# A fused convolution and expert layer: where one expert's sums are loaded, when kept weights, chunk stores, sends and ranks stand in the plan

## The chip, the core and the metric

One core of a Trainium2 chip runs the kernel: TensorE (PE, with PEld for its weight loads), VectorE (DVE), ScalarE (ACT), GpSimd (POOL) and SyncE (SP), which work in parallel and each take their own instructions strictly in order. The metric is the device time of one execution in microseconds (us); less is better. Transfers are issued by SP and ACT (direct ones) and by POOL (indirect ones, with a row number for each row).

## The reference

28672 rows of 192 numbers go through two stages.

```python
w = softmax(weight_gen, axis=-1)                       # (8, 3584, 8 heads, 7 taps)
out = einsum('bshk,bskhg->bshg', w, x_unf)             # causal convolution with 7 taps, own weights for each row
x = out.reshape(28672, 192)
do_compute = x @ w_skip > 0
e_idx = argmax(x[do_compute] @ w_gate)                 # one of 8 experts
h = maximum(xc[mask] @ w1[e], 0.0)                     # 192 -> 1024
y[mask] = gate_w[mask, None] * (h @ w2[e])             # 1024 -> 192
out[do_compute] = xc + y
```

## The kernel before, in words

The convolution runs in 64 steps of 448 rows; four steps make a chunk of 1792 rows, and there are 16 chunks. A step has two `band` multiplications on DVE (L356, from `rot`, the softmaxed taps), `conv` on PE (L375), copies on ACT (L382), transposes on PE (`back`, L390) and copies into `acc` on ACT (L404, L406). After the fourth step of a chunk, `logits` (L413), `choose` on DVE (L428 to L452, which ends with the one-hot tiles `oh` and `rc`), `rank` on PE (L463 to L467) and `place` on DVE (L482 to L502) give every row its place in the bucket of its expert. `answer` (L508) stores the whole chunk in the output from SP, and 16 `send` scatters by POOL (L515) write the chunk's rows into the buckets.

The expert part works on pairs of 128-row tiles. `fetch` loads a pair's rows (`xg`, L653) and, after the first eight pairs, its expert's weights (L667); `prep_rows` splits and transposes the rows (L680 to L708); `up` and `down` (L718, L738) are the matmuls; `put` (L749) scatters the results. The first eight pairs use the weights in the slot where an expert was prepared.

`prep_expert(e)` prepares an expert's weights in pieces, one piece at each token `P`: the largest absolute sums of the next expert's raw weights are measured on ACT (`measure`, L223), their 128x2 sums are written to DRAM from ACT's queue (`peaks`, L225), and two pieces later `spread` (L230) loads all sums back into every partition. One piece later `load_raw` loads the raw weights of the expert after that from ACT's queue (L209). The next `prep_expert` begins on DVE with the maximum over the loaded sums (L238) and a few small instructions, whose result scales the first weights on ACT (L252). `keep` (L277) stores a prepared expert in DRAM from SP, in three transfers, for later pairs.

`SEQ` is the plan: four strings, one for each step of a chunk, of one-letter tokens. The kernel walks them, and a token whose condition holds emits its instructions there; every engine keeps that order. `F` is a place of the expert pipeline: it moves the pair at work by half a stage, pops one scatter (`pop`), and deals five pending small DVE instructions. `R` emits `rank`, `r` what follows it, `W` starts `place`, `V` emits `answer`, `5` stores the taps to `img` (L344) and `4` loads them back as `rot` (L349), `x` loads the step's rows (L309), `s` emits `keep`, `D` emits `fetch`, `P` one piece of the preparation. Pairs begin at step 15 (`START`). When all chunks are placed and sent, the remaining pairs run alone.

Of the kernel before, what the change touches and what calls it, by code (L numbers as in the profile page):

```python
# [20 lines left out]
P = 128  # L21
B, S, D, H, K = 8, 3584, 192, 8, 7
G = D // H
# [33 lines left out]
]  # L57
# [11 lines left out]
FAST = 6  # L69
FIRST = 14  # L70
TT = 2
LAG = 2
# [4 lines left out]
def conv_moe_kernel(ctx, tc, x, wg, w_skip, w_gate, w, out):  # L77
    nc = tc.nc
# [15 lines left out]
    outs, unsent = [], []  # L94
# [110 lines left out]
    all_sums = spare.bitcast(F32)[:, 0:2 * P]  # L205
# [8 lines left out]
    def load_raw(e):  # L214
        if e < E:
            raws[e] = [load_part(e, i) for i in range(2)]
# [10 lines left out]
    def spread(e):  # L227
        if e < E:
            pk = peaks[e:e + 1, :]
            nc.sync.dma_start(all_sums, bass.AP(tensor=pk.tensor, offset=pk.offset, ap=[[0, P], [1, 2 * P]]))  # L230

# [47 lines left out]
    fresh, unkept = {}, []  # L279
    prepared, prepares = [0], [0]  # L280

    def prep_all():
        load_raw(0)
        yield
        measure(0, 0)
        yield
        measure(0, 1)
        load_raw(1)
        yield
        yield  # L290
        spread(0)
        yield
        for e in range(E):
            while e >= SLOTS and spent[0] <= e - SLOTS:
                yield
            yield from prep_expert(e)
            prepared[0] += 1
            yield
# [475 lines left out]
    step, tick = [0], [0]  # L774
# [103 lines left out]
    ffn = [None]  # L878
# [10 lines left out]
    n = dict.fromkeys("kOCGceKLlRrHhWiV", 0)  # L889
# [13 lines left out]
    def placed(c):  # L903
# [3 lines left out]
        n["i"] += 1  # L907

    def chosen(c):
        yield from choose(c)  # L910
        n["h"] += 1

    def assigned(own):
# [3 lines left out]
    def token(t, k):  # L917
# [6 lines left out]
        elif t == "F":  # L924
            advance(n["K"] > n["O"])
            for _ in range(FAST if not ffn[0] and n["i"] <= 3 else 1):
                pop()
# [7 lines left out]
        elif t == "s":  # L935
            if unkept and k >= FIRST:
                keep()
# [12 lines left out]
        else:  # L950
            i = n[t]
            c = i // NQ
# [11 lines left out]
                "H": lambda: (i < n["l"], lambda: chores.append(chosen(i))),  # L964
                "R": lambda: (i < n["h"], lambda: rank(i)),
                "r": lambda: (i < n["R"], lambda: rank_out(i)),
# [15 lines left out]
    with tc.manual_schedule():  # L982
# [33 lines left out]
        while n["V"] < NCHUNK or unsent or not last[0]:  # L1016
            k = n["k"]
# [63 lines left out]
```

## Time and profile before

| what | value |
|---|---|
| median of three runs | 983.23 us (978.15 to 986.6) |
| the profiled execution | 983.36 us, its span 981.6 us |
| PE busy | 803.0 us (82% of the span) |
| DVE busy | 663.9 us (68%) |
| ACT busy | 468.1 us (48%) |
| POOL busy | 398.3 us (41%) |
| mean granted TensorE clock | 0.927 |

PE is the busiest engine. Its busy share is low in the first third and high after it: the page gives it in 40 slices of 24.5 us as `0586534576767999898899989999998999999997`, and the clock that it was granted in the same slices as `9897566898888999999999999999998999999999`. So the views of single stretches tell more than the means.

### The profile page before, as it was taken

What the parts mean: (1) busy time and instruction counts of PE and PEld (TensorE: products, weight loads), DVE (VectorE), ACT (ScalarE), POOL (GpSimd) and SP (SyncE); (2) the same over time, 40 slices, a digit from 0 to 9 for tenths busy, and PEclk for the clock granted to TensorE, in tenths of its full rate; (3) what the DMA queues carried; (4) which work ended last, traced back from release to release, by engine and by line L of the source; (5) the groups of instructions that cost most, each with busy time, mean ns of one, the idle gap of its engine ahead of it and who ended that gap; (6) DMA issues with size and microseconds to landing.
All of it is one profiled execution on the core that took longest, in us unless ns stands there. A gap on an engine that the chain in (4) does not pass through costs nothing. (4 is left out here: it accounts for less than half of the span.)

```text
span 981.6 us, 36503 instructions
## 1 busy us (share of the span) xinstructions
PE 803.0 (82%) x15128; PEld 686.0 (70%) x15128; DVE 663.9 (68%) x1937; ACT 468.1 (48%) x1119; POOL 398.3 (41%) x417
## 2 busy tenths in 40 slices
PE   0586534776767999898899989999998999999997
PEld 0465323664656877687777877887886888889996
DVE  7597464866857688767668676867764666775553
ACT  1463352555544544455444555554544554454441
POOL 1028734142045544554254525352533545362222
PEclk9897566898888999999999999999998999999999
DMA  5957848867674849586676768674947384989990
GB/s 168 284 159 211 231 145 263 307 170 210 214 240 148 295 126 339 159 282 216 204 244 201 244 211 247 229 238 140 303 126 248 119 295 136 318 258 314 243 242 20
DMA packets 110793, 214.70 MB, mean 219 GB/s; under 512 B 28786, under 2 KB 68525, under 8 KB 108834
## 3 DMA queue, kind: packets, MB, share of 16 engines
q1 hardware_dynamic: 77794, 175.13, 54.7%
q10 hardware_dynamic: 15072, 15.48, 7.1%
q0 software_dynamic: 17760, 21.75, 7.1%
q8 instruction: 119, 1.95, 0.9%
q14 instruction: 48, 0.39, 0.1%
HBM read 141.37 MB, written 77.81 MB: 223 GB/s over the span
## 5 line engine op out<-in xcount | busy, mean ns | idle before, releaser
L515 POOL DMA_INDIRECT bucket<-acc,ixi x256 | 273.3, 1068 | 309.7 <-ACT hh L722 68.8
L718 PE MATMUL ph<-xT,wst 128*128 128x256 f16 x2280 | 297.3, 279 | 27.0 <-DVE hl L728 13.5
L718 PEld LDWEIGHTS <-wst 128*128 128x128 f16 x2280 | 220.4, 100 | 67.6 <-issue 28.5
L722 ACT ACTIVATE hh<-ph 128x512 f16<-128x512 f32 x228 | 135.7, 596 | 255.3 <-PE ph L718 241.3
L738 PE MATMUL py<-wst,hh 128*128 128x192 f16 x1824 | 249.0, 249 | 0.0
L738 PE MATMUL py<-wst,hl 128*128 128x192 f16 x912 | 226.7, 249 | 2.1 <-issue 1.9
L749 POOL DMA_INDIRECT out_dram<-xg x114 | 116.7, 1024 | 269.4 <-DVE xg L744 206.2
L728 DVE SCALAR_TENSOR_TENSOR hl<-ph,hh 128x512 f16<-128x512 f32 x228 | 155.2, 682 | 100.6 <-ACT hh L722 98.7
L356 DVE TENSOR_TENSOR bd<-rot,mask 128x896 f32<-128x896 f32 x128 | 137.3, 1081 | 62.8 <-PE bt L375 61.1
L375 PE MATMUL bt<-bd,xt 64*32 64x56 f32 x8192 | 128.9, 233 | 59.0 <-issue 23.0
L738 PEld LDWEIGHTS <-hh 128*128 128x128 f16 x1824 | 164.0, 99 | 17.5 <-issue 9.8
L375 PEld LDWEIGHTS bt<-bd,xt 64*32 64x32 f32 x8192 | 102.8, 113 | 92.8 <-issue 48.6
L390 PE MATMUL pa<-ident,xs 128*112 128x128 f32 x512 | 78.2, 299 | 25.1 <-ACT acc L404 10.9
L738 PEld LDWEIGHTS <-hl 128*128 128x128 f16 x912 | 90.2, 99 | 0.8 <-DVE hl L728 0.5
L390 PEld LDWEIGHTS pa<-ident,xs 128*112 128x112 f32 x512 | 64.0, 148 | 29.0 <-ACT xT L706 11.4
L744 DVE SCALAR_TENSOR_TENSOR xg<-py,fc,xg 128x192 f32<-128x192 f32 x114 | 42.2, 411 | 59.4 <-PE py L738 55.0
L382 ACT COPY xs<-bt 128x448 f32<-128x448 f32 x128 | 65.8, 539 | 31.6 <-PE bt L375 25.8
L706 ACT COPY xT<-pt 128x512 f16<-128x512 f16 x92 | 49.4, 589 | 43.1 <-PE pt L705 43.0
L689 ACT ACTIVATE xs<-xg,rs 128x192 f16<-128x192 f32 x114 | 45.5, 447 | 44.1 <-DVE rs L686 32.2
L404 ACT COPY acc<-pa 112x384 f32<-112x384 f32 x128 | 56.1, 482 | 8.9 <-PE pa L390 5.7
L705 PE MATMUL pt<-ident,xs 128*128 128x128 f16 x368 | 32.6, 227 | 22.3 <-DVE xs L695 8.8
L680 ACT ACTIVATE xs<-xg 128x192 f16<-128x192 f32 x114 | 40.2, 359 | 12.6 <-DMA xg<-bucket 10.7
(149 smaller groups left out, 700.0 us busy)
## 6 DMA issues: line engine op xcount, KB each, us to landing
wst<-wsp SPq DMA_DIRECT2D x98, 512.0 KB
wst<-wsp SPq DMA_DIRECT2D x49, 520.0 KB
xt<-in_x_dram SPq DMA_DIRECT2D x64, 384.0 KB
out_dram<-acc SPq DMA_DIRECT2D x16, 1358.0 KB
raw<-in_moe_w_dram ACTq DMA_DIRECT2D x16, 768.0 KB
xg<-bucket SPq DMA_DIRECT2D x57, 194.0 KB
wsp<-wst SPq DMA_DIRECT2D x16, 512.0 KB
rot<-img SPq DMA_DIRECT2D x16, 448.0 KB
```

Source lines behind the costliest of these rows:

```text
L356: nc.vector.tensor_tensor(bd.rearrange("p h (m u) -> p h m u", m=K), rot_[c][:, :, i0 * H:(i0 + 2) * H].rearrange("p m h -> p h m").unsque ...
L375: mm = nc.tensor.matmul(bt[a][GP * j:GP * (j + 1), c0:c0 + QH], xt[p0:p1, b0:b0 + GP], bd_[k, i // 2][p0:p1, i % 2 * H + h, :], start=True ...
L382: nc.scalar.copy(xs_[k][:, 2 * a:2 * a + 2, :], bt_[k][a][:, 0:2 * QB * QH].rearrange("p (x c) -> p x c", x=2))
L390: nc.tensor.transpose(pa[j][0:Q, x * P:(x + 1) * P], xs[:, x, j * Q:(j + 1) * Q], ident)
L404: nc.scalar.copy(acc_[c].rearrange("p (a b) d -> p a b d", a=2)[:, :, 2 * q + j, 0:D].rearrange("p a (h g) -> p a h g", g=G), pa[j][0:Q, : ...
L515: i = nc.gpsimd.indirect_dma_start(out=bviews[t], out_offset=bass.IndirectOffsetOnAxis(ap=rt_[c][:, t:t + 1], axis=0), in_=acc_[c][:, t, : ...
L706: nc.scalar.copy(xT[:, t], pt)
L718: mm = nc.tensor.matmul(ph[:, fi * 2 * P:(fi + 1) * 2 * P], wt[:, a * FF + f0:a * FF + f0 + P], xT[:, :, cc, :], start=j == 0, stop=j == 4)
L722: nc.scalar.activation(hh, ph, AF.Relu)
L728: nc.vector.scalar_tensor_tensor(hl, ph, 0.0, hh, op0=ALU.max, op1=ALU.subtract)
L738: mm = nc.tensor.matmul(py[:, t, 0:D], l[:, a], w2v[:, f, r, :], start=f == 0 and t == 0 and j == 0, stop=f == NFB - 1 and j == 2, skip_gr ...
L749: i = nc.gpsimd.indirect_dma_start(out=oviews[nsc[0] % 8], out_offset=bass.IndirectOffsetOnAxis(ap=xg[:, t0 + t, D + 1:D + 2].bitcast(I32) ...
```

## The change

Five things change. The load of the sums (`spread`) is issued from ACT's queue where it was SP's; for the first expert it also comes before the second expert's raw weights. Kept weights are stored from step 16 on (`KEEP`), where it was step 14 (`FIRST`, which still rules the pairs' assignment). `V` stands in the fourth string behind `4`, where it stood in the third ahead of `5`. A place pops two scatters while more than eight of a chunk are unsent. `R` waits until the place counter is past the one at which `choose` ended, by one place more when pairs are at work.

```diff
-    "x F C W r R a D P F G W r V P F W D 5 c b T M P F e P F P F D P s T M K O F P",
-    "x F C a D P F G 4 P F D c b T M P F e 0 P F P F D 1 P s T M K O F P",
+    "x F C W r R a D P F G W r P F W D 5 c b T M P F e P F P F D P s T M K O F P",
+    "x F C a D P F G 4 V P F D c b T M P F e 0 P F P F D 1 P s T M K O F P",
+KEEP = 16
-            nc.sync.dma_start(all_sums, bass.AP(tensor=pk.tensor, offset=pk.offset, ap=[[0, P], [1, 2 * P]]))
+            nc.scalar.dma_start(all_sums, bass.AP(tensor=pk.tensor, offset=pk.offset, ap=[[0, P], [1, 2 * P]]))
         measure(0, 1)
+        yield
+        spread(0)
+        yield
         load_raw(1)
-        yield
-        yield
-        spread(0)
         yield
     def chosen(c):
         yield from choose(c)
         n["h"] += 1
+        chosen_at[0] = tick[0]
-            for _ in range(FAST if not ffn[0] and n["i"] <= 3 else 1):
+            for _ in range(FAST if not ffn[0] and n["i"] <= 3 else 1 + (len(unsent) > 8)):
                 pop()
-            if unkept and k >= FIRST:
+            if unkept and k >= KEEP:
                 keep()
-                "R": lambda: (i < n["h"], lambda: rank(i)),
+                "R": lambda: (i < n["h"] and tick[0] > chosen_at[0] + (1 if ffn[0] else 0), lambda: rank(i)),
```

Line numbers of the kernel after are larger by one from L52 to L909, by three or four behind that.

The first place is ACT's order around the sums of expert 3 (`spare` is the tile that they are loaded into; `raw` here are the raw weights of expert 4). Before:

```order
L225 DMA peaks<-wm 128x2
L404 COPY acc<-pa 112x2x192 x2
L406 COPY ls<-pl 128x224
L459 ACTIVATE dl<-dl 112x128
L474 COPY qf<-rk 128x136
L209 DMA raw<-in_moe_w_dram 128x1536 x2
L382 COPY xs_2065<-bt 128x448
L252 ACTIVATE wst<-raw,wsc 128x1024
```

After, at the same place:

```order
L226 DMA peaks<-wm 128x2
L231 DMA spare<-peaks 128x256
L405 COPY acc<-pa 112x2x192 x2
L407 COPY ls<-pl 128x224
L460 ACTIVATE dl<-dl 112x128
L475 COPY qf<-rk 128x136
L210 DMA raw<-in_moe_w_dram 128x1536 x2
L383 COPY xs_2065<-bt 128x448
L253 ACTIVATE wst<-raw,wsc 128x1024
```

The load of the sums now stands on ACT, ahead of the raw weights and right behind the store that it waits for.

The second place is SP's order at steps 14 and 15, where the first pair's rows are fetched. Before:

```order
L508 DMA out_dram<-acc 112x3104
L344 DMA img_79<-wt 8x7x896 x2
L277 DMA wsp<-wst 128x2048 x2
L277 DMA wsp<-wst 128x2080
L309 DMA xt_134<-in_x_dram 128x768
L650 TENSOR_LOAD bs
L653 ISA
L653 DMA xg<-bucket 128x2x194
L349 DMA rot<-img_79 128x7x128
```

After:

```order
L345 DMA img_79<-wt 8x7x896 x2
L310 DMA xt_134<-in_x_dram 128x768
L651 TENSOR_LOAD bs
L654 ISA
L654 DMA xg<-bucket 128x2x194
L350 DMA rot<-img_79 128x7x128
L509 DMA out_dram<-acc 112x3104
```

The chunk's store moved behind the fetch and `rot`, and the first kept expert is no longer ahead of them.

The third place is PE's order at the rank of chunk 4, at the border of steps 20 and 21. Before, the rank stands between an `up` and a `down` stage:

```order
L718 MATMUL ph<-xT,wst 128x256
L463 LDWEIGHTS ones_89
L463 MATMUL rk<-oh_3783,ones_89 128x120
...
L467 LDWEIGHTS ones_89
L467 MATMUL rk<-rc,ones_89 128x8
L738 LDWEIGHTS hh
```

After, with the second half of the next step's convolution ahead of it:

```order
L719 LDWEIGHTS wst
L719 MATMUL ph<-xT,wst 128x256
L376 MATMUL bt<-bd,xt_135 32x56 x32
L464 LDWEIGHTS ones_89
L464 MATMUL rk<-oh_3666,ones_89 128x120
...
L468 LDWEIGHTS ones_89
L468 MATMUL rk<-rc,ones_89 128x8
L719 LDWEIGHTS wst
```

The rank moved two places back, behind work that does not need what it waits for.

## Rows read from the trace of the kernel before

**Rows 1.** Stretches: engines' busy us (instructions), clock, DMA share, GB/s.

```profile
95.00:176.00 81.00, 36.03 (x929) 27.19 (x929) 42.56 (x96) 35.55 (x66) 40.01 (x40) 0.61 0.72 214
176.00:300.00 124.00, 92.78 (x1680) 75.80 (x1678) 86.05 (x236) 64.41 (x133) 37.23 (x41) 0.89 0.68 218
300.00:791.00 491.00, 445.24 (x8783) 378.43 (x8759) 349.67 (x1064) 245.66 (x626) 222.32 (x223) 0.97 0.66 216
```

**Rows 2.** Waits, 95 to 300 us: who for whom, us in total, times, longest.

```profile
ACT wst L252 <- DVE wsc L243: 36.4, 6, 8.6
```

**Rows 3.** Timeline, expert 2's sums: start us, us, what, [idle before <-releaser].

```profile
104.18 0.33 ACTq L225 DMA_DIRECT2D peaks<-wm  x1
...
111.42 0.32 SPq L230 DMA_DIRECT2D spare<-peaks  x1
...
120.23 0.42 DVE L238 TENSOR_REDUCE wmv<-spare 128x2 f32<-128x256 f32 x1 [10.59 <-DMA spare<-peaks]
...
121.49 1.15 ACT L252 ACTIVATE wst<-raw,wsc 128x1024 f16<-128x1024 f32 x1 [8.60 <-DVE wsc L243]
...
122.92 0.98 PE L393 MATMUL pl<-xs,gt 128*32 128x224 f32 x8 [5.66 <-ACT L L421]
```

**Rows 4.** Timeline, expert 3's sums, and PE's next idle stretch.

```profile
128.77 0.33 ACTq L225 DMA_DIRECT2D peaks<-wm  x1
...
131.22 0.82 ACTq L209 DMA_DIRECT2D raw<-in_moe_w_dram  x2
131.71 0.33 SPq L230 DMA_DIRECT2D spare<-peaks  x1
...
140.48 0.42 DVE L238 TENSOR_REDUCE wmv<-spare 128x2 f32<-128x256 f32 x1 [4.32 <-DMA spare<-peaks]
...
149.25 1.95 PE L390 MATMUL pa<-ident,xs 128*112 128x128 f32 x8 [10.89 <-ACT acc L404]
```

**Rows 5.** Timeline, expert 5's sums, and PE's next idle stretch.

```profile
210.41 0.33 ACTq L225 DMA_DIRECT2D peaks<-wm  x1
...
214.47 0.34 SPq L230 DMA_DIRECT2D spare<-peaks  x1
...
223.35 0.42 DVE L238 TENSOR_REDUCE wmv<-spare 128x2 f32<-128x256 f32 x1 [1.73 <-DMA spare<-peaks]
...
229.41 1.10 PE L390 MATMUL pa<-ident,xs 128*112 128x128 f32 x4 [6.74 <-ACT xT L706]
```

**Rows 6.** Timeline, the sums of experts 4 and 7: store and load.

```profile
148.35 0.33 ACTq L225 DMA_DIRECT2D peaks<-wm  x1
...
152.66 0.33 SPq L230 DMA_DIRECT2D spare<-peaks  x1
...
256.49 0.33 ACTq L225 DMA_DIRECT2D peaks<-wm  x1
...
259.47 0.33 SPq L230 DMA_DIRECT2D spare<-peaks  x1
```

**Rows 7.** Timeline, the first kept expert and the first pair's rows.

```profile
161.13 4.12 SPq L277 DMA_DIRECT2D wsp<-wst  x3
...
165.35 1.31 SPq L309 DMA_DIRECT2D xt<-in_x_dram  x1
168.23 0.42 SPq L653 DMA_DIRECT2D xg<-bucket  x1
...
172.21 0.36 ACT L680 ACTIVATE xs<-xg 128x192 f16<-128x192 f32 x1 [10.71 <-DMA xg<-bucket]
```

**Rows 8.** PE's groups, 300 to 791 us: busy us, mean ns, idle before.

```profile
L463 PE MATMUL rk<-oh,ones 112*128 112x120 f16 (+4 forms) x150 | 6.9, 197 | 7.8 <-DVE oh L448 6.0 <-ACT dl L459 1.8
```

**Rows 9.** SP's waits, whole span: us in total, times, longest.

```profile
SPq L230 <- DMA peaks<-wm: 59.5, 7, 16.6
```

**Rows 10.** Timeline of ACT, the second expert's raw weights and their first use.

```profile
37.93 2.02 ACTq L209 DMA_DIRECT2D raw<-in_moe_w_dram  x2
...
61.94 1.47 ACT L223 ACTIVATE spare<-raw 128x1536 f16<-128x1536 f32 x1
```

More of the change, by code (lines that the diff above doesn't have):

```diff
@@ L287, in prep_all @@
         measure(0, 1)
-        load_raw(1)
-        yield
         yield
         spread(0)
+        yield
+        load_raw(1)
         yield
@@ L907, in placed @@
         n["i"] += 1
+    chosen_at = [0]
     def chosen(c):
```

## Prediction, made before the changed kernel was run

> **What bounds the kernel now.** I read the stretches first, then the waits of the weak stretches, then the timeline around the longest of them. From 300 to 791 us PE is busy 445.2 of 491 us at a granted clock of 0.97 [rows 1]: only 45.8 us are idle, so this part is bound by PE's work, and only a wait of PE itself is worth anything there. From 95 to 300 us it is different: PE works 128.8 of 205 us, at a clock of 0.61 and then 0.89 [rows 1], where 1 is 2.4 GHz and a half is 1.2 GHz. There the experts' weights are prepared, and engines wait for each other. The largest wait of ACT in that stretch is the first scaled weights (L252) for DVE's small chain: 36.4 us in six waits [rows 2]. The timeline shows what is behind three of them. For expert 2 the sums' store is issued at 104.18, SP issues the load at 111.42, DVE's maximum begins at 120.23 after 10.59 us of waiting for that load, ACT goes on at 121.49 after 8.60 idle us, and PE's next gap is 5.66 us [rows 3]. For expert 3 the same: load issued at 131.71, maximum at 140.48, and a PE gap of 10.89 us behind it [rows 4]. For expert 5: 214.47, 223.35 and a PE gap of 6.74 us [rows 5]. In all three the load of 128 KB takes 8.8 to 8.9 us from issue to use, and DVE, ACT and PE have nothing left to do meanwhile. So here time is lost in a chain of latencies, not in work.
>
> **The change part by part.**
>
> *Sums from ACT's queue.* Removed from SP: eight loads and 59.5 us of SP's waiting for the sums' store [rows 9]. That waiting itself I cost at nothing: at expert 3, for one, SP had issued what stood ahead, and PE's gap ends with ACT, not with a transfer. What counts is how long the load takes. At expert 3 ACT issues two loads of raw weights (768 KB each) at 131.22, and SP's load of the sums comes at 131.71, beside them [rows 4]. After the change ACT issues the sums first and the raw weights behind them; that is the first order listing. No row shows this load without the raw weights beside it. From below the nearest row is the sums' store at its shortest, 128.77 to 131.71, 2.9 us [rows 4]; from above it is the load itself, 8.8 us. In between, a small load (194 KB) from SP's queue that others are ahead of takes 168.23 to 172.21, 4.0 us [rows 7]. I take 4.0: it is the one row of a small load that stands beside other traffic and not behind 1.5 MB of it. The gain is 8.8 - 4.0 = 4.8 us for each of the experts 2, 3 and 5, 14.4 us in all, and PE's gaps behind them (5.66, 10.89, 6.74) are longer than 4.8 each, so I let all of it reach PE.
>
> The Trainium skill speaks against this part: its page "DMA: Bandwidth & Descriptors", section "Issuing engines are not separate DMA queues", says that transfers from any engine run on the same 16 DMA engines and interleave, so that another issuer saves only issue time. The trace agrees that they interleave, with the 8.8 us beside the raw weights; by the rule alone the 14.4 us would be nothing, and my sum would be 979.9.
>
> *What this adds to ACT.* ACT now waits for the sums' store, with its copies for PE queued behind. From store to load SP took 7.2, 2.9 and 4.1 us at experts 2, 3 and 5 [rows 3 to 5], and there ACT was idle later in the same chain anyway, so the wait only changes its place. At experts 4 and 7 no gain stands against it: 4.3 and 3.0 us [rows 6]. In both, copies for PE still stand ahead of the load and take a part of that time; how much no row shows. The bounds are nothing and 7.3 us, and I charge some 60%, 4.5 us. For the first expert the second one's raw weights come later; they were issued at 37.93 and first used at 61.94 [rows 10], 24 us and some four steps later; moved by two of these steps they still have about 12 us, more than the 8.8 above, and the steps between hide them. Nothing.
>
> *Kept weights and the chunk's store.* At step 14 and 15 SP spends 4.12 us on issuing the first expert's three transfers, then 1.31 on a load of rows that needs PE's progress, and the first pair's rows come at 172.21, when ACT has been idle for 10.71 us [rows 7]. After the change the kept weights and the chunk's store are not ahead of them (second listing). The load `xt` waits for PE in any case, so the 4.12 are no gain; I take 0.8 of its 1.31 and 1.2 of the 4.0 us of the landing (down to 2.9), 2.0 us. The kept weights then run beside steps 16 to 23. What hides them is that their slots are not rewritten before expert 4's preparation, about two steps later; if that cover is gone, expert 4 waits for 1.5 MB, 7 us at the 218 GB/s of that stretch [rows 1]. The chunk stores behind `rot` cost nothing while PE is the bound; one of them is 1.36 MB, 6.3 us at 216 GB/s, ahead of rows that are loaded three steps early.
>
> *Rank later.* From 300 to 791 us PE idles 7.8 us before the ranks' matmuls, nearly all of it for the one-hot rows [rows 8]. With two places of other work ahead (third listing) they should be over when PE arrives. The rank's own matmuls stay (6.9 us). Since PE is idle elsewhere in 9% of this stretch, I let 6.0 us reach the end and 1.8 be waited for elsewhere.
>
> *Two sends a place.* Scatters are moved, none added. POOL is busy 222.3 of 491 us [rows 1], and nobody waits for a send within a step. By the plan's own rules the last chunk is placed and sent one step earlier (476 places where there were 483) and one more pair lies inside the convolution's steps from step 31 on. PE's work is the same in both, so I cost this at nothing.
>
> **The sum.** 981.6 - 14.4 + 4.5 - 2.0 - 6.0 = 963.7 us of span. The profiled execution took 1.8 us more than its span (983.4), and stands 0.1 above the median of the runs. So 965.5 us.
>
> **The rivals.**
>
> *The rank's wait is refilled.* PE runs its stages in a fixed order, and two places later it may meet another late product of DVE. For it: DVE is busy 71% of that stretch (349.7 of 491) [rows 1]. Against it: the rank waits for ten small instructions at once, others for one. Then 6.0 us are missing: 971.5.
>
> *The sums come no faster.* If the load still takes 8.8 us because other traffic of SP slows it, the 14.4 us are gone and 979.9 is left. For it: expert 2's load had SP's own traffic around it, which stays. Against it: at expert 3 little but the raw weights was new, and they now come behind. This is what the skill's rule above gives.
>
> *ACT becomes the place where everything stops (slower).* The load needs 8.8 us, and ACT in addition waits for each store while it had work to do: 7.2 + 2.9 + 4.3 + 4.1 + 3.0 = 21.5 us [rows 3 to 6] that PE pays, less 2.0 and 6.0: 981.6 + 13.5 + 1.8 = 996.9. For it: at expert 3 the load is queued right behind the store (first listing), ahead of `acc` copies that PE waits for. Against it: ACT was idle in just those chains. It decides where ACT's added wait is not taken off the later one, that is, when the load takes as long as before.
>
> **How the numbers follow.** The forecast has a chance of 0.46, the refilled rank 0.20, no faster sums 0.21, ACT as the bottleneck 0.09, and 0.04 are for the kept weights in the way of steps 16 to 23. About 1% (9.8 us, 973.4 to 993.1) is what a measurement of this kernel can tell from no change. Faster: nearly all of the first (0.44), most of the second (0.15), a little of the third (0.03), together 0.62. Slower: most of the fourth and a part of the rest, 0.09. Same: 0.29. The range's lower end takes the load at 2.9 us (3 x 1.1 = 3.3), no added wait on ACT (4.5), the rank's 7.8 in full (1.8), and a granted clock that is back earlier: at 0.89 some 27 of the 124 us from 176 to 300 run at half rate [rows 1], and if a third of them goes, some 4.5 us of PE's time do. That is 14.1 below, 951.4, so 951. The upper end is the third case without the 2.0 us of the first pair, 981.9, so 982. For the forecast alone it is 951 to 971.
>
> **What would show it.** Right: L239, the maximum, begins within 5 us of ACT's issue of the sums for experts 2, 3 and 5; L253's wait for DVE falls from 36 to about 20 us; the first `up` of a pair comes some 10 us earlier; PE's idle time before L464 from 300 on is under 2 us; the clock from 95 to 300 is higher. Wrong: the load takes over 7 us still; ACT has idle stretches of 3 to 7 us in front of its copies with the sums' store as what ended them, and PE gaps right behind; measures that wait for raw weights, which are now issued later; PE's idle time from 300 on the same, under other lines.

## The result

The changed kernel takes 975.06 us (median of 19 runs, 966.73 to 984.39) where the kernel before takes 985.02 (19 runs, 978.15 to 989.86): a ratio of 0.9901, 95% interval 0.9874 to 0.9927. The ratios here and below are of the runs in the faster of two states in which the chip was found; the medians are of all runs. The forecast was 965.5: the sign was right, and 10 us came where 18 were forecast. The profiled execution has a span of 969.5 us, 12.1 less than the 981.6 of before.

The stretches of the changed kernel, columns as in [rows 1]:

```profile
95.00:176.00 81.00, 43.80 (x1021) 32.83 (x1022) 49.67 (x122) 39.90 (x80) 39.13 (x41) 0.60 0.71 211
176.00:300.00 124.00, 85.12 (x1660) 70.14 (x1661) 83.60 (x224) 63.02 (x130) 48.88 (x47) 0.85 0.73 234
300.00:791.00 491.00, 450.47 (x8789) 386.75 (x8786) 352.20 (x1070) 247.30 (x629) 222.93 (x219) 0.98 0.67 220
```

From 95 to 176 us PE is busy 7.8 us more than before, and from 176 to 300 it is 7.7 us less: in busy time, what was gained by 176 is given back by 300. Of its matmuls, 92 more lie before 176 and 20 fewer behind it. The granted clock was 0.60 and 0.85, and not higher than the 0.61 and 0.89 of before. From 300 to 791 its idle time is 40.5 us where it was 45.8.

The waits from 95 to 300 us (who for whom, us in total, times, longest):

```profile
ACT wst L253 <- DVE wsc L244: 15.0, 4, 4.3
DVE wmv L239 <- DMA spare<-peaks: 14.5, 2, 9.5
ACT acc L405 <- DMA peaks<-wm: 11.0, 2, 7.2
```

ACT's wait for the scaled weights' factors has fallen from 36.4 us [rows 2] to 15.0, and a wait for the sums' store stands in its place. The timeline shows the three chains of [rows 3 to 5] again. Expert 2, expert 3 and expert 5, each from the store (L226) and the load (L231) to the maximum (L239), with ACT's and PE's idle stretches behind:

```profile
102.54 0.33 ACTq L226 DMA_DIRECT2D peaks<-wm  x1
...
111.36 0.35 ACTq L231 DMA_DIRECT2D spare<-peaks  x1
...
113.20 0.95 ACT L334 ACTIVATE wt<-wt 112x896 f32<-112x896 f32 x1 [9.31 <-issue]
...
114.56 3.19 PE L414 MATMUL lt<-four,ls 128*112 128x32 f32 x16 [6.72 <-ACT acc L405]
...
116.82 0.42 DVE L239 TENSOR_REDUCE wmv<-spare 128x2 f32<-128x256 f32 x1 [9.52 <-DMA spare<-peaks]
```

```profile
125.36 0.33 ACTq L226 DMA_DIRECT2D peaks<-wm  x1
...
128.34 0.33 ACTq L231 DMA_DIRECT2D spare<-peaks  x1
...
129.61 0.98 PE L464 MATMUL rk<-oh,ones 112*128 112x120 f16 x15 [9.13 <-ACT acc L405]
...
135.65 0.41 DVE L239 TENSOR_REDUCE wmv<-spare 128x2 f32<-128x256 f32 x1
```

```profile
201.99 0.33 ACTq L226 DMA_DIRECT2D peaks<-wm  x1
...
209.80 0.34 ACTq L231 DMA_DIRECT2D spare<-peaks  x1
210.18 0.48 ACT L405 COPY acc<-pa 112x384 f32<-112x384 f32 x1 [7.22 <-DMA peaks<-wm]
...
212.56 2.29 PE L719 MATMUL ph<-xT,wst 128*128 128x256 f16 x10 [8.01 <-DVE hl L729]
...
219.34 0.41 DVE L239 TENSOR_REDUCE wmv<-spare 128x2 f32<-128x256 f32 x1
```

From the store's issue to the maximum it is 14.28, 10.29 and 17.35 us, 41.9 in all; before it was 16.05, 11.71 and 12.94, 40.7 [rows 3 to 5]. The three chains together have not become shorter at all, although the loads have: by the landings that the traces record, they took 5.4, 4.6 and 7.7 us from their issue, where it was 8.7, 8.8 and 8.9, 8.7 us less in all. Two things took that back. From the stores to the loads it is 5.4 us more in all (8.8, 3.0 and 7.8 us, before 7.2, 2.9 and 4.1). And at experts 3 and 5 the maximum begins 2.8 and 1.8 us after the load has landed: its rows show no idle time of DVE, which was still at other work. PE's idle stretches near these chains (6.72, 9.13 and 8.01) are about what they were (5.66, 10.89 and 6.74).

What did become earlier is the first pair. SP's and ACT's rows there, to be held against [rows 7]:

```profile
141.94 1.44 SPq L345 DMA_DIRECT2D img<-wt  x2
143.48 0.53 SPq L310 DMA_DIRECT2D xt<-in_x_dram  x1
161.11 0.41 SPq L654 DMA_DIRECT2D xg<-bucket  x1
...
163.69 0.36 ACT L681 ACTIVATE xs<-xg 128x192 f16<-128x192 f32 x1 [2.54 <-DMA xg<-bucket]
...
167.65 1.52 SPq L278 DMA_DIRECT2D wsp<-wst  x3
```

The load `xt` of a later step's rows is issued at 143.48 and not at 165.35, the pair's rows at 161.11 and not at 168.23, the kept weights behind them, and ACT waits 2.54 us for the rows where it waited 10.71. The first `hh` (L723) of a pair comes at 171.0 us, before at 179.5 (L722).

Between `xt` and the pair's rows SP now stands for something else. From 140 to 176 us its longest wait is for the scatters that write the chunk's rows into the buckets:

```profile
SPq L654 <- DMA bucket<-acc,ixi: 14.2, 1, 14.2
```

The last of the 16 scatters ahead of the fetch, in the kernel before and in the changed one:

```profile
158.34 1.67 POOL L515 DMA_INDIRECT bucket<-acc,ixi  x1 [0.30 <-issue]
```

```profile
156.69 1.33 POOL L516 DMA_INDIRECT bucket<-acc,ixi  x1 [0.31 <-issue]
```

By the recorded landings it was down at 165.65 before and at 160.89 after. So the 8.5 us by which ACT gets the rows earlier are 1.7 from the scatter's earlier start, 3.1 from its landing (4.2 us where it was 7.3), 2.4 from the fetch, which now follows 0.2 us behind the landing and followed 2.6 us behind it, and 1.4 from the rows' own load.

PE's groups from 300 to 791 us, columns as in [rows 8]:

```profile
L719 PE MATMUL ph<-xT,wst 128*128 128x256 f16 x1311 | 169.5, 277 | 28.8 <-DVE hl L729 20.1 <-issue 4.1 <-ACT xs L383 3.2
...
L464 PE MATMUL rk<-oh,ones 112*128 112x120 f16 (+4 forms) x150 | 7.2, 200 | 0.0
```

The 7.8 us before the ranks are gone; before L719 PE now waits 28.8 us, where the same row of the kernel before (L718) had 16.7:

```profile
L718 PE MATMUL ph<-xT,wst 128*128 128x256 f16 x1260 | 164.2, 279 | 16.7 <-DVE hl L728 9.6 <-ACT xs L382 2.7 <-issue 1.7
```

Where the 12.1 us of span lie is read off the start of each pair's first `hh`, after against before: 8.5 us earlier at the first pair, 6.4 at the tenth (352 us before), 12.1 at the last. So 8.5 were won by the first pair, 2.1 lost by the tenth, 5.7 won behind it. This is one execution of each kernel, and between the tenth pair and the last the difference goes up to 18.1: parts of a few us depend on the pair at which one cuts.

### The profile page after: what moved, and what is told of

The parts are those of the page before. It is cut to its first block, busy times and chain, and to the rows that moved or that the text cites. A ratio compares the mean times of both kernels' runs of the same rounds, so it can differ in the third digit from the quotient of the medians.

```text
span 969.5 us, 36517 instructions
## 1 busy us (share of the span) xinstructions
PE 800.5 (83%) x15128; PEld 685.7 (71%) x15128; DVE 663.9 (68%) x1937; ACT 467.3 (48%) x1119; POOL 406.6 (42%) x417
## 3 DMA queue, kind: packets, MB, share of 16 engines
q8 instruction: 119, 1.95, 0.9%
## 5 line engine op out<-in xcount | busy, mean ns | idle before, releaser
L516 POOL DMA_INDIRECT bucket<-acc,ixi x256 | 279.3, 1091 | 259.3 <-DVE bb L624 99.2
L719 PE MATMUL ph<-xT,wst 128*128 128x256 f16 x2280 | 295.6, 278 | 43.1 <-DVE hl L729 28.8
L719 PEld LDWEIGHTS <-wst 128*128 128x128 f16 x2280 | 219.8, 100 | 83.4 <-issue 41.9
L723 ACT ACTIVATE hh<-ph 128x512 f16<-128x512 f32 x228 | 135.5, 596 | 256.7 <-PE ph L719 250.2
L750 POOL DMA_INDIRECT out_dram<-xg x114 | 119.0, 1044 | 299.5 <-DVE xg L745 254.9
L376 PE MATMUL bt<-bd,xt 64*32 64x56 f32 x8192 | 126.5, 231 | 63.4 <-DVE bd L357 22.6
L376 PEld LDWEIGHTS bt<-bd,xt 64*32 64x32 f32 x8192 | 100.7, 112 | 96.5 <-issue 43.2
L383 ACT COPY xs<-bt 128x448 f32<-128x448 f32 x128 | 66.1, 539 | 35.5 <-PE bt L376 20.6
L706 PEld LDWEIGHTS <-xs 128*128 128x128 f16 x368 | 24.1, 99 | 26.4 <-ACT xs L690 13.8
```

The source lines that it names most:

```text
L376: mm = nc.tensor.matmul(bt[a][GP * j:GP * (j + 1), c0:c0 + QH], xt[p0:p1, b0:b0 + GP], bd_[k, i // 2][p0:p1, i % 2 * H + h, :], start=True ...
L383: nc.scalar.copy(xs_[k][:, 2 * a:2 * a + 2, :], bt_[k][a][:, 0:2 * QB * QH].rearrange("p (x c) -> p x c", x=2))
L516: i = nc.gpsimd.indirect_dma_start(out=bviews[t], out_offset=bass.IndirectOffsetOnAxis(ap=rt_[c][:, t:t + 1], axis=0), in_=acc_[c][:, t, : ...
L706: nc.tensor.transpose(pt[:, 2 * i2 + i, :], xs[:, t, i2, i * P:(i + 1) * P], ident16)
L719: mm = nc.tensor.matmul(ph[:, fi * 2 * P:(fi + 1) * 2 * P], wt[:, a * FF + f0:a * FF + f0 + P], xT[:, :, cc, :], start=j == 0, stop=j == 4)
L723: nc.scalar.activation(hh, ph, AF.Relu)
```

## The experiments

The runs were taken in six groups, and each group has its own runs of the kernel before, which the ratios are against. In two groups the kernel before took 980 and 982 us, as it did where the forecast was measured; in the other four it took 1114 to 1131 us, with more idle time of PE that the profile gives to "issue" (shown below), and the edits are worth something else there. What sets the kind of group no run shows (the chips' numbers do not: 3 occurs in both). I call them 980 groups and 1115 groups.

| label | kernel before, us | ratio | 95% interval |
|---|---|---|---|
| b_sums, b_sums_2 | 1114.5, 1130.8 | 1.0076, 1.0033 | 1.0044 to 1.0108, 0.9998 to 1.0068 |
| b_sums_3 | 981.5 | 0.9984 | 0.9944 to 1.0024 |
| b_rank, b_rank_2 | 1114.5, 1130.8 | 0.9943, 0.9923 | 0.9912 to 0.9974, 0.9882 to 0.9964 |
| b_keep | 1114.5 | 0.9971 | 0.9927 to 1.0014 |
| b_sends | 1114.5 | 1.0296 | 1.0255 to 1.0336 |
| after_again | 1115.6 | 1.0486 | 1.0419 to 1.0554 |
| a_send1, a_send1_2, a_send1_3 | 1125.6, 1115.6, 1130.8 | 0.9966, 0.9975, 1.0000 | 0.9938 to 0.9994, 0.9945 to 1.0005, 0.9963 to 1.0037 |
| a_sums_sp | 1125.6 | 1.0441 | 1.0389 to 1.0494 |
| a_keep14 | 1125.6 | 1.0418 | 1.0354 to 1.0482 |
| a_rank_old | 1125.6 | 1.0265 | 1.0216 to 1.0313 |
| b_quiet | 980.1 | 1.0019 | 0.9975 to 1.0062 |
| a_quiet | 980.1 | 0.9911 | 0.9870 to 0.9952 |
| s1_pemax | 1130.8 | 0.9883 | 0.9822 to 0.9944 |
| s1_pemax_2 | 981.5 | 0.9871 | 0.9817 to 0.9925 |

### The sums' edit alone, and undone

In the kernel before (labels b_), and the reverse in the changed kernel (a_sums_sp):

```diff
-            nc.sync.dma_start(all_sums, bass.AP(tensor=pk.tensor, offset=pk.offset, ap=[[0, P], [1, 2 * P]]))
+            nc.scalar.dma_start(all_sums, bass.AP(tensor=pk.tensor, offset=pk.offset, ap=[[0, P], [1, 2 * P]]))
...
         measure(0, 1)
+        yield
+        spread(0)
+        yield
         load_raw(1)
-        yield
-        yield
-        spread(0)
         yield
```

> The kernel before with the first edit alone: the sums are loaded back from ScalarE's queue, the second expert's raw weights come behind the first sums. Theory A (the forecast's: the load gets faster, 14.4 us saved and 4.5 us of new waits paid): about 10 us faster, 975 against 985, and each load takes about 4 us. Theory B (from the trace of the changed kernel, where the loads took 4.6 to 8.5 us): the load still shares the transfer engines with the raw weights that ACT issues right behind it; loads of 5 to 7 us for experts 2 to 4, no gain for 5 to 7, together 2 to 6 us faster. Theory C (ACT becomes the bottleneck): slower by 5 us or more, with ACT idle in front of its copies for the sums' store.

> The kernel before with the first edit alone, again. Where the kernel before takes about 980 us: theory A (the forecast's, loads of 4 us): 0.990; theory B (loads of 5 to 8.5 us, as in the changed kernel): 0.994 to 0.999; theory C (ACT becomes the bottleneck): 1.005 or more, as the 1.008 on the chip where the kernel before took 1114 us.

> The kernel before with the first edit alone. Where the kernel before takes about 980 us: theory A (the forecast's, loads of 4 us): 0.990; theory B (loads of 5 to 8.5 us, as in the changed kernel): 0.994 to 0.999; theory C (ACT becomes the bottleneck): 1.005 or more. Where it takes over 1100 us: 1.003 to 1.008, as twice before.

> The changed kernel with its first edit undone: the sums come back from SP's queue, the second expert's raw weights ahead of the first sums. Theory A (the forecast's): about 10 us slower than the changed kernel, so a ratio to the kernel before of 1.00. Theory B (the loads of the changed kernel took 4.6 to 8.5 us, those of experts 2 to 4 gained, those of 5 to 7 lost): within 4 us of the changed kernel, 0.987 to 0.995. Theory C (the queue of ACT does harm): faster than the changed kernel, under 0.987.

In the 980 group the edit alone gives nothing that can be told from no change: 0.9984, at most 5.5 us by the interval, where 9.9 were forecast for it (14.4 less 4.5). In the 1115 groups it costs 0.8 and 0.3 per cent, the second not clear of nothing. Undone in the changed kernel it gave 1.0441, no better and no worse than the changed kernel's own 1.0486 in another 1115 group. So theory A is out; in the 980 group the result lies between B and nothing. Why the first pair does not come earlier with this edit alone is seen in SP's rows of b_sums_3 (its profiled execution took 988.2 us, the median of its runs is 983.3; the order and the waits are read here):

```profile
146.33 0.53 SPq L508 DMA_DIRECT2D out_dram<-acc  x1
146.91 2.49 SPq L344 DMA_DIRECT2D img<-wt  x2
149.44 6.69 SPq L277 DMA_DIRECT2D wsp<-wst  x3
161.87 0.34 SPq L309 DMA_DIRECT2D xt<-in_x_dram  x1
168.87 0.42 SPq L653 DMA_DIRECT2D xg<-bucket  x1
```

```profile
SPq L267 <- ACT low L254: 6.2, 1, 6.2
SPq L653 <- DMA bucket<-acc,ixi: 5.7, 3, 3.6
SPq L309 <- DMA spare<-peaks: 5.7, 1, 5.7
SPq L277 <- DMA out_dram<-acc: 3.9, 1, 3.9
```

SP no longer waits for the sums' store, but the chunk's store and the kept weights still stand ahead of `xt` and of the first pair's rows, which come at 168.87 us; in the kernel before it was 168.23. What holds the rows at the end is not the queue, though, but the scatters (L653): the last one is down at 168.65, 8.2 us after its start at 160.49, and the fetch is issued 0.2 us behind it. In the kernel before SP's queue is held by the wait for the sums' store; its waits from 140 to 176 us there begin with

```profile
SPq L230 <- DMA peaks<-wm: 11.2, 1, 11.2
SPq L344 <- DMA spare<-peaks: 2.9, 1, 2.9
SPq L309 <- DMA spare<-peaks: 2.6, 1, 2.6
```

So `xt` stood behind two things, the wait for the sums' store and the block of stores, and taking away the first alone only brings the second to light. The pair's rows need the scatters besides, and an earlier place in SP's queue is worth nothing to them before the last scatter has landed.

### Kept weights alone, and undone

With `KEEP` 16 in the kernel before, and `KEEP` 14 in the changed kernel for a_keep14:

```diff
-            if unkept and k >= FIRST:
+            if unkept and k >= KEEP:
```

> The kernel before with the second edit alone: the kept weights are stored two steps later. Theory A (the forecast's): the first pair's rows come 2 us earlier and all of it is kept, 2 us faster. Theory B: what the first pair gains, the later small transfers lose, since the stores of 1.5 MB an expert now run beside the sums' stores and loads of experts 5 to 7 (in the changed kernel these took 15.5, 12.1 and 9.4 us where they had taken 12.9, 10.4 and 7.3): between 2 us faster and 3 us slower.

> The changed kernel with its second edit undone: the kept weights are stored from step 14 on. Theory A (the forecast's): 2 us slower than the changed kernel, 0.992. Theory B: the kept weights no longer run beside the sums' stores and loads of experts 5 to 7; those get 2 us shorter each, and the first pair's rows come later by 2 us: within 3 us of the changed kernel.

Alone 0.9971 with an interval on both sides of 1, undone 1.0418 against 1.0441 for another part undone in the same group: nothing that these runs can tell, and both were 1115 groups. What the moved stores do in a 980 group is read from rows alone. The first `hh` comes 0.7 us earlier than before with the sums' edit (b_sums_3), and 8.0 and 8.5 us earlier in the two kernels that have both edits and `V` behind `rot` (a_quiet, below, and the changed kernel). The last scatter lands 7.3, 7.7 and 8.2 us after its start in the kernel before, b_quiet and b_sums_3, and 4.2, 4.7 and 2.9 in the changed kernel, a_quiet and s1_pemax_2 (below). In the kernel before 1.4 MB of the chunk's store moved in that time, in the changed kernel none of it. That the stores' traffic is what made the scatter late fits these six traces; it was not tested alone (in b_sums_3, 1.6 MB of raw weights moved instead). Kept weights and `V` were not taken apart, nor from the other edits that these kernels share.

### The rank's edit alone, and undone

```diff
+        chosen_at[0] = tick[0]
...
-                "R": lambda: (i < n["h"], lambda: rank(i)),
+                "R": lambda: (i < n["h"] and tick[0] > chosen_at[0] + (1 if ffn[0] else 0), lambda: rank(i)),
```

> The kernel before with the last edit alone: a rank is taken a place later (two places beside a pair). Theory A (the forecast's): the 7.8 us of PE's idle time before the ranks from 300 us on go, 6 us faster. Theory B: the wait goes, but the plan changes too: the place at which no pair is under way moves from step 23 to step 20, so the pair behind it starts about 20 us later as in the changed kernel, and 0 to 3 us are left. Theory C (the wait is refilled by another late product): no change, with PE's idle time from 300 us on as before.

> The kernel before with the last edit alone, again. Where the kernel before takes about 980 us: theory A (the forecast's): 6 us faster, 0.994, as on the chip where the kernel before took 1114 us; theory B (the place without a pair moves to step 20 and takes a part back): 0.997 to 1.000; theory C (the wait is refilled): 1.000.

> The changed kernel with its last edit undone: a rank is taken as soon as it may be. Theory A (the forecast's): PE waits 6 to 8 us before the ranks again, 6 us slower than the changed kernel, a ratio to the kernel before of 0.996. Theory B: the wait comes back, but the place without a pair moves from step 20 to step 23 and the fourth pair starts some 15 to 20 us earlier; within 3 us of the changed kernel, 0.987 to 0.993.

Alone it gives 6.4 and 8.7 us (0.57 and 0.77 per cent) in two 1115 groups, each clear of 1. Its trace (the first row) has no idle time before L463 from 300 to 900 us, where that of b_keep (the second), which ranks as before, has 6.6:

```profile
L463 PE MATMUL rk<-oh,ones 112*128 112x120 f16 (+4 forms) x150 | 7.3, 202 | 0.0
```

```profile
L463 PE MATMUL rk<-oh,ones 112*128 112x120 f16 (+4 forms) x150 | 6.9, 197 | 6.6 <-DVE oh L448 4.6 <-ACT dl L459 2.0
```

Theory A has it, although theory B's mechanism is there too: by the plan the place without a pair moves from step 23 to step 20 in each kernel with this rule. In the 980 groups it was not run alone; there the three kernels that have it (the changed one, a_quiet, s1_pemax_2) win 5.7, 7.9 and 3.9 us between the tenth pair and the last, and the two that have not (b_quiet, b_sums_3) lose 1.3 and 0.3, one execution each. Undone beside two scatters a place it is 1.0265, better than the 1.0441 and 1.0418 of its group: there the later rank costs, and why no run shows.

### Two scatters a place, alone and undone

```diff
-            for _ in range(FAST if not ffn[0] and n["i"] <= 3 else 1):
+            for _ in range(FAST if not ffn[0] and n["i"] <= 3 else 1 + (len(unsent) > 8)):
```

> The kernel before with the fourth edit alone: two scatters a place while more than eight of a chunk are unsent. Theory A (the forecast's): no difference, within 1 us. Theory B: the plan has no longer the place at step 30 at which no pair is under way, and one pair more lies inside the convolution's steps from 31 on; since PE is idle where a pair does not stand beside a step, 3 to 6 us faster.

> The changed kernel as it is, for reference on the chip of this call. Where the kernel before takes about 985 us: 0.990, all theories. Where it takes over 1100 us, with PE waiting for its own instructions in the blocks of L376: theory A (the two scatters a place cost the same there whatever else is changed): 1.02 to 1.03, since the fourth edit alone gave 1.030 and the whole without it 0.997; theory B (the edits depend on each other): 0.99 as on the first chip.

> The changed kernel with its fourth edit undone: one scatter a place. Theory A (the forecast's): no difference, 0.990 against the kernel before. Theory B: the place without a pair at step 30 comes back and one pair less lies inside the convolution's steps, 3 to 6 us slower than the changed kernel, 0.993 to 0.996. Theory C: two scatters a place get in the way of other transfers, and one is better, under 0.987; another chip, on which the kernel before took 1114 us with PE waiting for its own instructions, showed the edit alone 3 per cent slower.

> The changed kernel with the fourth edit undone, one scatter a place, beside the whole. Where the kernel before takes about 985 us: theory A (two scatters a place are free): 0.990; theory B (they close the place without a pair at step 30): 0.993 to 0.996; theory C (they cost there too, less): under 0.987. Where it takes over 1100 us: 0.997 as before.

> The changed kernel with the fourth edit undone, again, beside the kernel of the next run. Where the kernel before takes about 980 us: theory A (two scatters a place are free there): 0.990; theory B (they close the place without a pair at step 30): 0.993 to 0.996; theory C (they cost there too): under 0.987. Where it takes over 1100 us: 0.997, as twice before.

In 1115 groups this edit alone costs 3.0 per cent, and with it the changed kernel is 4.9 per cent slower than the kernel before; with one scatter a place the same kernel is level (0.9966, 0.9975, 1.0000). What they do in a 980 group stays open, since a_send1 and b_sends met none. What differs in these groups is seen in PE's waits over the whole span: the changed kernel in its own profile, a_send1_2, and after_again, which is the changed kernel again, in this order:

```profile
PE bt L376 <- issue: 22.0, 14, 5.6
```

```profile
PE bt L376 <- issue: 107.3, 190, 4.9
```

```profile
PE bt L376 <- issue: 122.5, 208, 4.3
```

"issue" is a wait for nothing that the profile shows; that PE's own instructions come late is a reading of it, and no run shows it directly. It falls in the blocks of 64 band matmuls, a dense part of PE's program. I took each block from 300 to 900 us in two halves of 32 and measured from the first start to the last. In the kernel before a half takes 0.30 us on average where GpSimd sends no scatter meanwhile, and 0.48 where it sends for over half of the time; in a_send1_2 it is 0.30 and 1.33, in after_again 0.34 and 2.07. So in these groups PE's dense blocks are slow just while scatters are sent. PE's granted clock is lower, too; from 500 to 700 us in a_send1_2 and in after_again (columns as in [rows 1]):

```profile
500.00:700.00 200.00, 171.15 (x3250) 142.63 (x3249) 130.12 (x384) 89.43 (x226) 79.70 (x83) 1.00 0.64 210
```

```profile
500.00:700.00 200.00, 167.54 (x2800) 135.28 (x2798) 112.87 (x337) 77.35 (x195) 65.30 (x70) 0.87 0.52 174
```

PE is busy nearly as long (167.5 and 171.2 us) and does 2800 matmuls instead of 3250, at a granted clock of 0.87 instead of 1.00, a mean of stretches at 1.2 and at 2.4 GHz. That scatters and slow blocks go together is measured; that the one makes the other was to be settled by the next pair.

### Scatters kept away from the blocks

A rule is added to the kernel before (b_quiet) and to the changed one (a_quiet; `> 2` there): no scatter at the two places right ahead of a block. PE's order stays the same.

```diff
-            for _ in range(FAST if not ffn[0] and n["i"] <= 3 else 1):
+            for _ in range(FAST if not ffn[0] and n["i"] <= 3 else 0 if quiet[0] and ffn[0] else 1 + (len(unsent) > 4)):
...
+            row = SEQ[k % NQ].split()
+            for at, t in enumerate(row):
+                quiet[0] = t == "F" and next(u for u in row[at + 1:] + ["F"] if u in "FCG") in "CG"
```

> The kernel before, with one rule added: at the two places a step that stand right ahead of a block of 64 band matmuls (L375) no scatter is sent while pairs are at work, and at the other places two while more than four of a chunk are unsent. TensorE's order is the same to the last matmul, and so is the number of scatters. Theory A (while GpSimd sends a scatter, PE's dense blocks run short of instructions: in the runs so far half a block took 0.30 us without a scatter, and beside one 0.48 on the first chip and 1.3 to 2.1 on those where the kernel before takes over 1100 us): half blocks of about 0.3 us throughout; on a chip of the slow kind 70 to 150 us faster, on one like the first 10 to 30 us faster. Theory B (blocks and scatters only happen to coincide, the instructions come late by themselves): no change, 0.99 to 1.01. Theory C (scatters bunched into fewer places make rows late, as the fourth edit seemed to): slower, 1.02 or more.

> The changed kernel with the same rule added (two scatters at the other places while more than two of a chunk are unsent); TensorE's order is that of the changed kernel to the last matmul. Theory A: as fast as or faster than the kernel before with the rule, on either kind of chip, since what the fourth edit cost there was scatters lying on the blocks. Theory B: as the changed kernel, 1.05 on a chip of the slow kind, 0.99 on one like the first. Theory C: slower than the changed kernel.

This was a 980 group: 1.0019 and 0.9911, the latter level with the changed kernel's 0.9901. Theory A's 10 to 30 us did not come, but the edit did not do what it was to do either: of 152 half blocks 86 still lie beside a scatter for over half of their time (87 of 154 before), since GpSimd runs behind its places. The cause stays open. What the pair does show is the changed kernel's gain a second time, with the same profile (first `hh` of a pair 8.0 us earlier, 8.2 at the tenth pair, 16.1 at the last).

### The sums without store and load

This is a_send1 (one scatter a place), but the sums do not pass through memory: store and load are gone, and `spread2` comes a step of the preparation later, ahead of `load_raw`.

```diff
+    def spread(e):
...
+            tp = ps_s.tile([P, 512], F32, tag="s", name="tp")
+            nc.tensor.transpose(tp[0:2, 0:P], sums.pop(e), ident)
+            nc.vector.tensor_reduce(m2, tp[0:2, 0:P], AX.X, ALU.max)
...
+    def spread2(e):
...
+            nc.vector.tensor_scalar(d2, ident[0:2, 0:2], m2, None, op0=ALU.mult)
...
+            nc.tensor.matmul(bp[:, 0:2], ones2, d2, start=True, stop=True)
...
+            nc.vector.tensor_scalar(mv, bp[:, 0:2], 1e-30, None, op0=ALU.max)
```

> The kernel of the run above, but the experts' sums no longer go through memory: TensorE transposes the 128x2 sums, VectorE takes the maxima, one small matmul spreads them to all partitions; store and load of the sums are gone. Theory A (the chain of latencies from the sums' store to the first scaled weights is what the stretch from 95 to 300 us loses time in, and the change of queue took little of it): ACT's wait of L253 for VectorE falls under 10 us, and the kernel is 8 to 20 us faster than the run above. Theory B (the chain only hides other waits, for the raw weights above all): within 4 us of the run above. Theory C (TensorE now waits for the sums): slower than the run above.

> The kernel with one scatter a place whose sums go through TensorE and not through memory, again. Where the kernel before takes about 980 us: theory A (what the stretch from 95 to 300 us loses is the chain of latencies, which is gone): 0.975 to 0.985, faster than the changed kernel's 0.990; theory B (the gain of 1.2 per cent that it brought on the other kind of chip was TensorE's clock there): 0.988 to 0.995. Where it takes over 1100 us: 0.988 as before.

In the 1115 group it is 10.8 us faster than a_send1_3 beside it (1118.68 and 1129.48), in the 980 group 0.9871, the least of all. In that group's trace the first pair's `hh` comes 11.2 us earlier than in the kernel before, the tenth 15.3 (8.5 and 6.4 in the changed kernel). Its stretches and waits from 95 to 300 us:

```profile
95.00:176.00 81.00, 46.69 (x1134) 35.70 (x1134) 53.86 (x136) 40.91 (x82) 37.06 (x39) 0.64 0.68 218
176.00:300.00 124.00, 95.77 (x1718) 79.05 (x1717) 87.39 (x248) 67.93 (x144) 50.14 (x47) 0.86 0.67 231
```

```profile
PE tp L232 <- ACT acc L421: 22.6, 3, 8.3
...
ACT wst L267 <- DVE wsc L258: 13.8, 4, 4.1
...
PE tp L232 <- ACT spare L224: 12.8, 3, 6.3
```

PE is busy 142.5 us of these 205 us, where it was 128.8 before [rows 1] and 128.9 in the changed kernel; of its matmuls, 2852 lie there, where it was 2609 and 2681. So theory A's direction is right: the chain through memory held a part of this stretch. Its size is not: 12.7 us of the 15 to 25 that it expected, since PE itself now waits 35.4 us for ACT at the transposes, as theory C has it. This kernel is ahead of the kernel before in both kinds of group (0.9883, 0.9871). Ahead of the changed one it is clearly in 1115 groups (1.0486 there), where one scatter a place has a part in that; in 980 groups 0.9871 and 0.9901 have intervals that overlap, and the two were not run side by side.

## Why the prediction was right and wrong

**What bounds the kernel.** Right in the main: up to 300 us chains of waits bound it, and s1_pemax_2, which cuts one, is 8.9 us ahead of the changed kernel by the tenth pair (one execution each, of two groups); behind that it is PE's own work and waits.

**The sums' load, 14.4 us.** Wrong, and the term that the forecast failed by. The step that failed is that 4.8 us at each of three experts are gained and that "I let all of it reach PE". The loads did get faster by 8.7 us in all (5.4, 4.6 and 7.7 us to landing, where 4.0 was taken), but the stores ahead of them took 5.4 us more, DVE came 4.6 us later to the maximum, and the chains are 41.9 us where they were 40.7. b_sums_3 puts the whole edit at 1.6 us faster, with an interval from 5.5 faster to 2.4 slower. Two rows of before spoke against the step: DVE had stood for the load only 4.32 us at expert 3 and 1.73 at expert 5 [rows 4, 5], so "nothing left to do meanwhile" was not so, and no more than that could be won there.

The size rested on "no row shows this load without the raw weights beside it". That is not so either: expert 7 has none beside it, and its load [rows 6] landed 4.3 us after its issue. Over the eight loads of each of the two kernels it is 4.3 and 4.6 us where 0.3 to 0.4 MB moved in all meanwhile, and 7.4 to 9.1 us where 2.3 to 3.0 MB did, from SP's queue and from ACT's. A longer load also counts more bytes, so this shows that the two go together and no more. At expert 5 of the changed kernel, 1.4 MB of it was a chunk's store. The row of the 4.0 us was misread as well: the kept weights, 1.5 MB, are issued just ahead of it [rows 7]. That 4.0 came near the 4.6 of expert 3 is in part luck.

The page "DMA: Bandwidth & Descriptors" of the Trainium skill, section "Issuing engines are not separate DMA queues", would have had nothing come of this part. The 0.9984 agrees with that; the prediction had put that case at 0.21.

**ACT's added waits, 4.5 us.** Their size cannot be told. ACT now has idle stretches of 9.31, 3.75, 6.22, 7.22 and 1.47 us that hold the waits for the stores of experts 2, 3, 4, 5 and 7, 28.0 in all (some 1.8 of the 9.31 lie behind the load's issue). At L253 it waits 21.4 less for DVE, but 5.36 more at expert 6, which the view gives to "issue" and which ends with the load of the sums (below). So it is 6.6 or 12.0 more, and what of that reaches PE no run shows. "There ACT was idle later in the same chain anyway" does not hold at expert 5, where copies for PE were queued behind the load and PE stands 8.01 us. The rival in which ACT stops everything had such rows for its sign: in part it is there.

**Kept weights and the chunk's store, 2.0 us.** Too small: the first `hh` comes 8.5 us earlier, 7.7 more than with the sums' edit alone. The forecast had the rows' own load (1.2, measured 1.4) and a piece of SP's queue (0.8, measured 2.4 from the last scatter's landing to the fetch). It had no term for the scatters, which the fetch waits for: they are 1.7 us earlier and their landing is 3.1 us shorter. "Nobody waits for a send within a step" left that out, since SP stands 14.2 us for them. "The load `xt` waits for PE in any case" is refuted by its issue at 143.48, but `xt` is not what the pair waited for. Nor does the 11.2 us for which SP stood for the sums' store show as a gain: at 152.66 the last scatter was still 13 us from landing.

**Lost behind it, 2.1 us.** Not foreseen. With the later rank the place without a pair lies at step 20, and the fourth pair starts 20.6 us later than before. Most is caught up by the sixth pair (0.7). There the changed kernel has PE's longest idle stretch behind the first matmul; that it is a part of the 2.1 is not shown:

```profile
231.51 0.35 ACTq L231 DMA_DIRECT2D spare<-peaks  x1
...
240.04 0.42 DVE L239 TENSOR_REDUCE wmv<-spare 128x2 f32<-128x256 f32 x1 [5.01 <-DMA spare<-peaks]
...
241.34 1.15 ACT L253 ACTIVATE wst<-raw,wsc 128x1024 f16<-128x1024 f32 x1 [5.36 <-issue]
...
250.61 1.01 PE L706 MATMUL pt<-ident,xs 128*128 128x128 f16 x8 [14.01 <-ACT acc L405]
```

The load of expert 6's sums takes 8.5 us to the maximum, ACT stands for it, and then works through the whole preparation before the copies that PE waits for.

**The rank, 6.0 us.** Borne out, as far as the runs go: 6.4 and 8.7 us alone, in 1115 groups. In the 980 groups there is only the 5.7 behind the tenth pair, from one execution of each kernel; counted from the seventh it would be 2.3. The rival that the wait is refilled was half there (L719's idle time rose by 12.1 us), and still the sum of PE's idle time from 300 to 791 us fell by 5.2.

**Two scatters a place, nothing.** Not settled for groups like the forecast's. In the others it is the largest term of all, 3 to 5 per cent slower, with PE's idle time in the dense blocks, of which the profile of before showed little (23.0 us).

**The sum.** 981.6 - 8.5 + 2.1 - 5.7 = 969.5 us is the span that was measured; it comes out because its terms are pieces of that difference, and it confirms nothing. The forecast's terms up to the tenth pair were 14.4 - 4.5 + 2.0 = 11.9; 6.4 came, most of it by a way that the forecast did not have.

## To carry to other kernels

Cost a wait in a queue by what stands behind it at the one place where somebody is short of it, and then ask what else that one waits for: here the first pair's rows stood in SP's queue, but they needed the last of 16 scatters as well. A small transfer that others wait for does not get fast by another queue while bulk transfers move beside it; take it off that way. A gain ahead of an engine reaches it only as far as the engine was idle for it, so read the idle time in its own row first. A plan that is better by its places should also be run where PE's dense blocks are slow, before it is called free.

## What the hardware showed beyond that

The same program took some 980 us in two groups and 1114 to 1131 in four, at a granted clock of 0.91 to 0.94 and of 0.87 to 0.90. The changed kernel took 975 and 1168 us, with 22.0 and 122.5 us of PE's waits given to "issue". The Trainium skill's page "Runtime: NRT & Kernel Launch", section "Instruction fetch mechanics", calls the cost of going from one block of instructions to the next mostly hidden. Whether that is what PE waits for here no run shows; the instructions' queue moves the same 119 packets, 1.95 MB, in both.

A transfer can wait for another that it has nothing to do with: in b_sums_3 SP's `xt` waits 5.7 us until ACT's load of the sums has landed, and reads and writes other memory. In the trace both count their landing on the same semaphore, and the transfers of both queues share eight semaphores. In this program two queues are not two independent lines.
